# The written-out order of a two-stage attention and MoE kernel, listed anew

## The chip, the cores and the metric

The kernel runs on one core of a Trainium2 chip, as one launch. The metric is the device time in microseconds; the kernel before takes 568.86 us as the median of three runs (568.36 to 571.24).

## What is computed

The inputs are `q`, `k`, `v`, `a_re`, `a_im` of shape 4 x 8 x 768 x 48 (batch, heads, sequence, head size) and two weight matrices of 384 x 2048 and 2048 x 384. The first stage is a linear recurrence over the sequence with a complex decay, the second an MLP on all 3,072 tokens:

```python
mag = sqrt(a_re**2 + a_im**2); scale = minimum(mag, 0.999) / (mag + 1e-6)
for t in range(S):
    S_re, S_im = ar * S_re - ai * S_im + k[t] outer v[t], ar * S_im + ai * S_re
    y[t] = q[t] @ S_re
x = y, with the heads of a token side by side      # 3072 x 384
h = x @ w_in
out = (h * sigmoid(1.702 * h)) @ w_out
```

## The kernel before, in words

The tokens are cut into 12 **chunks** of 256 (`u`, 0 to 11), and the chunks into seven **groups** (`GROUPS`, line 39: chunk 0, chunk 1, then pairs). For each chunk `prepare` (from line 281) turns the decays into factors: a load of `ri` (line 324), logarithms and exponentials on ScalarE (lines 329 to 334), an arctangent (line 351), scans on VectorE (lines 356, 376, 396), sines (lines 424, 425), and the rotation of `qk` into `qr` and `qk` (line 229, steps "rot0" and "rot1"). Each rotated tensor is then brought into the layout by heads, `qkh`, in a **remap**: five DMAs on-chip (lines 447, 448, 450). `attend` (from line 454) computes the chunk's scores on TensorE (line 511), masks them on VectorE into `pm` (line 517), turns keys (line 530, copied out by ScalarE in line 534), mixes the values (line 501) and carries a state `st` from chunk to chunk (lines 553, 569; its decay, line 472, reads the last column of the remapped tensor). The result goes to `xhi` and `xlo` (lines 559, 563). `moe` (from line 617) multiplies by `w_in` into `h_ps` (line 650), applies the activation on ScalarE (lines 659; 663 and 665), takes the rest of it on VectorE into `gl` (line 667), multiplies by `w_out` into `o_ps` (line 681) and writes out through `osb` (line 699, DMA of line 702).

The weights come as float64 in 16 loads of 768 KB, f0 to f15 (line 245), through four buffers, and are **converted** in four steps each: lines 247, 250 and 254 on VectorE, line 253 on ScalarE. Group 0 multiplies in plain fp32 with the converted weights; the later groups take three fp32r products from a high and a low part, which a later split makes (lines 265 to 272). Beside this, the kernel looks at its inputs to see whether the fast way holds for them: 40 **reloads for a check** bring pieces of the weights and of `a` into `raw_w` (lines 710 and 731), and VectorE reduces each (lines 715; 732 and 735). One buffer serves all 40, so a reload waits until the check of the one before it has been done.

**What sets the order.** No scheduler runs. Every step above is a call of `add` in `Plan` (lines 62 to 87), numbered from 0 to 1737 in the order of the calls, with its engine, the tiles it reads and writes, and so the steps it depends on. `ORDER` (line 995) is a list of all 1738 numbers; the loop at line 878 emits the steps in that order. Every engine takes its own steps strictly in listed order, and waits where a step's inputs or buffers aren't ready, with all that is listed behind it on that engine. All DMAs are issued by SyncE (SP), in listed order as well, and a DMA that must wait holds those behind it. Before an activation that needs another table, line 881 emits a table load.

The numbers that are spoken of below:

| step | what it is |
|---|---|
| 80, 128 / 301 / 445 / 970, 1381 | loads of `ri`: chunk 0 (halves) / 1 / 2 / 6, 9 |
| 0, 5, 10, 15, 20, 25, 30, 35, 40, 45, 50, 55, 60 | weight loads f0, f1, f2 and so on to f12 |
| 8, 33, 38, 48 | ScalarE's part of a conversion (line 253) of f1, f6, f7, f9 |
| 100, 150 / 321 | loads of `qk`: chunk 0 (halves) / 1 |
| 164, 179 / 783 | loads of `v`: chunk 0 (both blocks) / 5 |
| 95 | arctangent (line 351) of chunk 0, first half |
| 105, 143, 108, 109 | ScalarE's steps behind the arctangent: lines 404, 351 (second half), 419, 424 |
| 113 | rotation "rot1" of chunk 0, first half; the 13 warm-up matmuls (line 432, steps 114 to 126) and remap 127 need it |
| 112, 127 / 161, 163 | remaps of chunk 0, first / second half |
| 331, 334 / 333, 336 | rotations / remaps of chunk 1 |
| 166, 168 / 181, 183 / 340, 342 | masks (line 517): chunk 0, first / second block / chunk 1 |
| 178 | decay of the state (line 472) by what remap 163 brings |
| 187, 190, 211 | chunk 0, second block: first mix on TensorE, copy of the result, first matmul of line 650 on it |
| 24, 200 | last step of the conversion of f4 (line 254); matmul of line 681 that needs it |
| 14, 29 | last steps of the conversions of f2 and f5; f6 and f9 go into the buffers that they free |
| 129 to 137 | ScalarE's and VectorE's steps on the second half of chunk 0 |
| 272 | split of the second weight tile (line 272) |
| 809, 818 / 887, 896 | `gl` on VectorE (line 667) and the matmul group of line 650 that waits for it: group of chunks 4 and 5, third / last step |
| 328, 329, 330 / 447 / 206, 271 | ScalarE: lines 419, 424, 425 of chunk 1 / line 205 of chunk 2 / activation (line 659) of chunk 0, split (line 265) |
| 1191, 1195 | copy of keys by ScalarE (line 534) in chunk 8, and the scores that wait for it |
| 1610 and 1736 | first `osb` copy of the last group; the matmul of line 753 that counts the checks |

Of the kernel before, what the change touches and what calls it, by code (L numbers as in the profile page):

```python
# [992 lines left out]


ORDER = """
80 5 10 128 100 15 150 0 103 164 81 82 84 83 85 86 6 87 7 88 89 92 90 94
91 11 93 96 95 12 104 129 102 130 97 105 131 132 99 134 135 16 136 106 137 140 133 101
141 138 142 139 107 144 301 143 1 108 153 109 145 154 111 146 110 149 18 112 98 8 155 113
148 157 158 156 152 114 127 147 151 303 2 115 159 3 9 116 302 117 160 13 118 304 25 161
119 17 120 305 4 121 122 307 162 123 165 306 19 169 308 166 35 163 167 309 315 124 171 168  # L1000
310 14 170 28 26 172 173 313 311 174 27 20 125 30 314 175 312 126 317 176 193 316 338 29
177 202 179 321 445 194 178 45 324 182 180 203 318 325 181 204 183 195 36 326 184 205 21 186
320 185 33 187 38 196 23 37 188 22 191 31 189 197 327 322 271 198 24 328 199 32 329 40
355 200 447 323 190 34 206 211 48 39 201 319 330 212 46 55 50 331 213 446 214 43 220 41
332 215 448 333 221 207 42 222 449 334 216 451 229 47 217 335 452 336 218 44 450 208 56 453
209 49 58 223 457 219 454 57 458 230 51 231 59 65 60 210 459 232 224 455 192 238 52 239
456 461 225 460 339 467 75 341 340 226 342 233 337 227 53 66 343 462 68 54 246 344 67 345
247 70 501 273 248 470 285 348 275 353 69 526 277 234 61 471 240 466 464 228 465 78 235 63
241 62 346 242 472 347 354 473 350 71 356 463 64 73 255 469 474 236 349 502 237 468 503 249
357 281 76 358 351 72 250 256 360 77 251 359 269 352 257 476 475 252 366 361 79 477 505 362  # L1010
504 363 74 253 507 478 258 508 243 364 506 245 270 479 509 365 254 510 515 368 511 513 244 367
512 514 517 369 259 481 291 498 260 272 295 261 518 263 262 274 516 377 522 482 523 676 484 483
370 378 519 485 371 265 297 267 486 372 299 373 276 488 374 521 527 487 375 379 496 520 491 480
528 524 386 380 529 279 387 278 531 376 525 532 489 490 381 283 534 388 493 382 389 678 383 530
280 535 533 384 282 494 385 395 677 536 287 396 390 391 537 397 284 289 392 393 398 286 404 679
405 497 680 399 394 293 288 400 681 401 290 413 682 292 414 690 402 406 492 407 403 294 499 415
699 416 540 545 408 409 417 495 422 691 692 410 500 737 411 702 538 683 539 684 296 542 546 541
543 560 266 268 264 412 685 688 431 547 686 544 548 687 689 693 423 550 549 703 558 298 551 552
694 698 555 432 424 556 696 418 697 695 704 559 419 425 420 300 706 553 701 433 1614 561 739 554
421 434 562 427 707 426 563 700 428 564 429 705 435 708 430 557 437 565 709 738 566 567 740 710  # L1020
571 741 568 1615 438 569 742 570 436 711 743 573 744 441 572 1616 579 439 574 1617 714 712 443 575
576 577 580 751 581 752 578 585 745 1618 582 746 1619 591 749 1620 909 444 750 753 583 747 763 748
440 584 754 760 717 731 586 592 715 587 589 713 593 588 758 764 716 597 756 765 718 755 590 594
598 719 759 595 721 599 757 911 761 603 766 762 720 1621 910 724 1622 604 600 722 1623 767 729 596
768 769 605 609 912 770 913 730 723 1624 915 1625 726 725 916 732 1626 771 601 917 918 606 772 602
914 615 919 923 920 733 921 607 610 922 935 611 926 727 608 734 1627 613 925 612 728 929 736 614
1628 735 924 1629 621 927 970 936 616 932 773 622 774 930 617 937 780 618 777 931 623 619 798 783
1630 620 781 627 938 624 782 775 934 628 784 629 1631 940 633 933 1632 941 776 972 939 943 625 942
928 971 785 944 626 630 634 631 778 1633 635 779 945 786 632 974 639 973 975 1634 788 1635 946 976
637 787 984 977 791 636 796 789 640 638 645 1636 986 996 643 646 1637 641 790 797 647 1638 997 793  # L1030
792 799 642 948 648 644 978 649 979 982 1639 794 650 980 985 651 981 983 795 1148 993 1640 800 1641
987 801 652 950 653 802 998 803 655 999 988 804 654 991 951 992 657 805 663 658 995 989 1150 1642
1000 1643 656 949 1644 947 990 442 659 661 994 1001 660 664 952 1003 665 806 1149 1002 1151 953 662 1645
954 807 1646 962 666 808 1647 1004 957 1005 955 669 1152 812 1154 1006 1155 1648 668 963 674 667 809 956
813 965 814 959 818 966 670 1156 672 958 1157 810 964 675 1017 815 1153 811 1162 967 816 819 960 968
961 1171 824 969 1649 820 1160 1650 1158 1163 1161 1159 817 821 1014 1165 1164 1007 822 1174 823 1651 830 1175
1166 1170 1009 831 1015 1008 825 1652 826 1011 1653 832 1205 827 1018 1169 1010 828 836 1654 1019 829 837 833
1020 1655 834 1022 1656 1012 1168 1013 1167 1021 842 1173 838 1016 1176 1030 1207 1657 1025 839 1177 835 1172 843
840 1179 1031 1658 844 1659 1032 848 1178 1180 1023 849 1033 845 1206 1181 1024 850 1660 1027 1661 841 1208 1209
846 1662 671 851 1211 1182 860 1212 1213 1034 1183 1026 1214 847 1215 1035 854 1028 1216 1231 1037 1029 1036 1210  # L1040
1043 673 1038 1044 1039 855 1663 856 852 857 1664 1219 1665 866 861 1217 862 1228 1218 1222 1040 1221 1186 1188
1232 853 858 1223 1233 863 1189 859 1220 864 867 1234 868 872 869 1184 1666 1667 865 873 1187 1668 1185 870
874 1230 1227 871 1190 876 1192 1229 1236 1669 1041 878 1237 1235 875 1670 1224 1238 1239 1671 1381 877 1225 879
884 1191 1241 880 1240 1200 1042 885 881 886 1195 1226 1193 1242 882 1382 883 1383 888 1384 1672 890 1385 1201
887 896 891 892 889 1194 1203 1196 1197 1673 1245 1198 893 1674 1202 1404 894 897 1199 898 899 895 901 1387
902 1388 1675 900 1386 1204 1045 1676 1389 1677 1390 1393 907 1243 1394 905 1244 908 903 1046 1247 1395 1391 904
1251 1250 1051 1047 1392 1246 1252 1678 1048 1049 1052 1398 1053 1050 1679 1055 1054 1397 1680 1248 1253 1401 1249 1057
1407 1396 1063 1058 1402 1681 1255 1682 1400 1254 1399 1683 1408 1403 1056 1064 1256 1257 1059 1258 1065 1060 1263 1409
1061 1264 1066 1411 1684 1412 1062 1406 1067 1685 1405 1686 1442 1069 1414 1068 1415 1070 1260 1071 1266 1072 1075 1410
1259 1687 1688 1267 1689 1265 1081 906 1076 1413 1261 1416 1077 1268 1073 1078 1262 1074 1417 1082 1087 1444 1269 1270  # L1050
1443 1079 1083 1084 1080 1445 1088 1085 1089 1690 1271 1446 1276 1093 1448 1277 1691 1090 1692 1419 1465 1418 1086 1094
1099 1449 1091 1450 1420 1422 1100 1272 1095 1101 1273 1421 1092 1274 1423 1097 1096 1451 1105 1447 1456 1098 1102 1106
1424 1454 1107 1111 1457 1426 1452 1275 1425 1453 1455 1693 1459 1427 1434 1458 1103 1468 1104 1112 1108 1109 1462 1113
1460 1435 1694 1429 1464 1695 1428 1437 1431 1110 1117 1696 1114 1466 1115 1118 1467 1469 1116 1119 1123 1120 1470 1697
1121 1698 1436 1124 1463 1471 1122 1125 1129 1473 1126 1472 1474 1127 1130 1131 1128 1430 1475 1135 1132 1438 1476 1133
1136 1137 1477 1278 1138 1439 1279 1134 1432 1440 1141 1441 1280 1140 1281 1139 1144 1290 1699 1433 1142 1146 1284 1282
1478 1291 1485 1285 1292 1283 1486 1286 1288 1287 1700 1296 1701 1488 1143 1289 1297 1479 1298 1299 1482 1480 1489 1481
1294 1702 1293 1490 1302 1487 1703 1704 1308 1303 1483 1491 1295 1492 1705 1304 1300 1305 1484 1301 1309 1314 1493 1310
1494 1496 1501 1306 1502 1311 1706 1307 1707 1147 1320 1312 1495 1321 1315 1504 1322 1498 1316 1313 1318 1323 1708 1317
1332 1709 1505 1710 1319 1326 1324 1327 1461 1328 1325 1329 1333 1330 1334 1497 1499 1711 1335 1331 1338 1344 1339 1340  # L1060
1341 1336 1337 1345 1350 1346 1347 1712 1713 1145 1503 1342 1343 1351 1356 1352 1353 1714 1348 1500 1715 1716 1362 1357
1358 1506 1507 1508 1717 1349 1718 1509 1719 1510 1354 1359 1355 1363 1360 1364 1365 1368 1361 1369 1366 1370 1371 1511
1367 1512 1372 1513 1374 1514 1720 1373 1375 1517 1379 1377 1721 1515 1722 1378 1518 1519 1516 1520 1521 1523 1723 1522
1524 1529 1525 1526 1535 1530 1531 1532 1724 1527 1725 1380 1528 1536 1541 1537 1538 1533 1534 1542 1547 1543 1544 1539
1540 1548 1545 1549 1550 1726 1546 1553 1551 1554 1555 1559 1556 1727 1728 1376 1552 1560 1565 1561 1557 1729 1562 1730
1558 1566 1731 1571 1567 1568 1563 1577 1572 1573 1564 1569 1574 1732 1583 1578 1579 1570 1575 1580 1576 1584 1581 1585
1586 1733 1582 1589 1595 1590 1591 1592 1734 1587 1735 1588 1596 1601 1597 1598 1593 1594 1602 1599 1603 1604 1600 1605
1606 1608 1736 1607 1610 1609 1611 1612 1737 1613
"""


# [66 lines left out]
```

## Time and profile before

| what | us |
|---|---|
| median of three runs | 568.86 (568.36, 568.86, 571.24) |
| the profiled execution, its own time | 570.0 |
| span in the profile, first to last instruction | 568.3 |
| outside the span, in that execution | 1.7 |
| first matmul | 23.90 |
| end of the last matmul | 561.98 |

How to read it: the page gives each engine's busy time as a share of the span. A share is a mean over the whole span, so the stretches have to be looked at by themselves. A wait is put down to what came last before the waiting instruction started. A matmul's end is modelled, so TensorE's busy time has small holes closed; PEld is the load of weights, which runs beside the matmul before it.

### The profile page before, as it was taken

The numbers are of one execution on the slowest core, as the hardware profiler recorded it, in microseconds if no ns is written. First come the engines' busy times: TensorE is split into PE (matmuls) and PEld (weight loads), VectorE is DVE, ScalarE is ACT, GpSimd is POOL, SyncE is SP. The second block draws the span as 40 slices with busy tenths as digits, with TensorE's granted clock in tenths as the row PEclk, the third lists the DMA queues.
The fourth block names the chain that finished last, engine by engine and source line by source line (L and its number), as shares of the span: only waits on it lengthen the run. The fifth ranks groups of instructions, "written<-read, shape, count | busy, mean of one in ns | idle before, by whom it ended". The sixth has DMA issues, their size and how long they took to land.

```text
span 568.3 us, 14533 instructions
## 1 busy us (share of the span) xinstructions
PE 529.1 (93%) x6204; PEld 447.7 (79%) x6204; DVE 388.6 (68%) x625; ACT 370.7 (65%) x562; POOL 11.1 (2%) x55
## 2 busy tenths in 40 slices
PE   0388999999999999989999999999999999999995
PEld 0267989999987888867888788888888888888884
DVE  6989999999989896967669659728653232241222
ACT  7978989999997969696485777498422133222230
POOL 6000000000000000000000000000000000000000
PEclk9999999999999999999999999999999999999999
DMA  8498983756284765575384753760253213111201
GB/s 337 136 275 314 225 336 66 220 111 203 56 240 141 192 198 128 185 163 163 127 221 125 189 184 107 201 186 1 88 111 88 65 29 89 43 47 47 75 0 60
DMA packets 29270, 82.04 MB, mean 144 GB/s; under 512 B 4112, under 2 KB 7184, under 8 KB 29200
## 3 DMA queue, kind: packets, MB, share of 16 engines
q1 hardware_dynamic: 29200, 81.06, 49.2%
q8 instruction: 50, 0.82, 0.6%
q14 instruction: 20, 0.16, 0.1%
HBM read 57.41 MB, written 4.72 MB: 109 GB/s over the span
## 4 chain that ended last, share of the span: by engine, by line
PE 58%; ACT 5%; DVE 5%; DMA 4%; issue 1%; ACTq 0%; POOL 0%; DVEq 0%
PE o_ps L681 25%; PE h_ps L650 24%; PE x_ps L501 4%; DMA raw_w<-in_w_in_dram 2%; PE z_ps L511 1%; PE p_ps L511 1%; PE z_ps L553 1%; DMA ri<-in_a_dram 1%; DMA qkh<-qr 1%; ACT L881 1%; DVE s L376 1%; DVE fit L715 1%; DVE s L356 1%; PE p_ps L530 1%; PE z_ps L530 1%
## 5 line engine op out<-in xcount | busy, mean ns | idle before, releaser
L663 ACT ACTIVATE gh<-h_ps 128x512 fp32r<-128x512 f32 x88 | 52.1, 597 | 144.3 <-PE h_ps L650 79.5
L667 DVE TENSOR_TENSOR gl<-h_ps,gh 128x512 fp32r<-128x512 f32 x88 | 60.1, 685 | 85.0 <-ACT h_ps L665 65.2
L650 PE MATMUL h_ps<-xhi,hiA 128*128 128x512 f32 (+1 forms) x288 | 109.2, 379 | 2.6 <-DVE gl L667 2.5
L650 PE MATMUL h_ps<-xhi,loA 128*128 128x512 f32 (+1 forms) x288 | 107.2, 372 | 0.0
L650 PE MATMUL h_ps<-xlo,hiA 128*128 128x512 f32 (+1 forms) x288 | 107.2, 372 | 0.0
L681 PE MATMUL o_ps<-gh,hiU 128*128 128x512 f32 (+1 forms) x288 | 80.9, 381 | 0.0
L681 PE MATMUL o_ps<-gl,hiU 128*128 128x512 f32 (+1 forms) x288 | 80.1, 379 | 0.4 <-DVE gl L667 0.4
L681 PE MATMUL o_ps<-gh,loU 128*128 128x512 f32 (+1 forms) x288 | 78.3, 372 | 0.0
L881 ACT ACT_TABLE_LOAD x59 | 75.7, 1283 | 1.9 <-PEq L1126 0.9
L650 PEld LDWEIGHTS h_ps<-xhi,hiA 128*128 128x128 f32 x288 | 54.2, 188 | 13.9 <-DVE gl L667 4.4
L650 PEld LDWEIGHTS h_ps<-xhi,loA 128*128 128x128 f32 x288 | 54.2, 188 | 9.8
L650 PEld LDWEIGHTS h_ps<-xlo,hiA 128*128 128x128 f32 x288 | 54.3, 188 | 9.0
L681 PEld LDWEIGHTS o_ps<-gh,loU 128*128 128x128 f32 x288 | 52.2, 188 | 9.7
L681 PEld LDWEIGHTS o_ps<-gl,hiU 128*128 128x128 f32 x288 | 51.1, 188 | 10.8 <-issue 1.2
L681 PEld LDWEIGHTS o_ps<-gh,hiU 128*128 128x128 f32 x288 | 50.7, 188 | 10.1 <-issue 1.2
L665 ACT ACTIVATE h_ps<-h_ps 128x512 f32<-128x512 f32 x88 | 51.6, 593 | 0.0
L715 DVE TENSOR_REDUCE fit<-raw_w 128x1 f32<-128x384 f32 x64 | 34.1, 544 | 17.0 <-DMA raw_w<-in_w_in_dram 10.3
L229 DVE TENSOR_TENSOR qk<-qk,s 128x768 f32<-128x768 f32 (+2 forms) x39 | 44.2, 1137 | 1.5 <-ACT s L425 1.3
L501 PE MATMUL x_ps<-pm,v 128*32 128x128 f32 x768 | 38.9, 276 | 1.8 <-DMA v<-in_v_dram 1.1
L501 PE MATMUL x_ps<-qkh,st 96*32 96x128 f32 x640 | 32.9, 272 | 0.0
L432 PE MATMUL h_ps<-qk,ident 128*128 128x256 f32 x26 | 7.9, 457 | 23.9 <-DVE s L415 23.9
L501 PEld LDWEIGHTS x_ps<-pm,v 128*32 128x32 f32 x768 | 20.0, 109 | 9.5 <-issue 6.0
(104 smaller groups left out, 783.0 us busy)
## 6 DMA issues: line engine op xcount, KB each, us to landing
v<-in_v_dram SPq DMA_DIRECT2D x24, 416.0 KB, 4.8
ri<-in_a_dram SPq DMA_DIRECT2D x11, 768.0 KB, 5.5
qk<-in_qk_dram SPq DMA_DIRECT2D x11, 768.0 KB, 6.7
qkh<-qr SPq DMA_DIRECT2D x22, 288.6 KB, 5.9
qkh<-qk SPq DMA_DIRECT2D x22, 288.6 KB, 5.6
raw<-in_w_in_dram SPq DMA_DIRECT2D x8, 768.0 KB, 6.7
raw<-in_w_out_dram SPq DMA_DIRECT2D x8, 768.0 KB, 6.3
raw_w<-in_w_in_dram SPq DMA_DIRECT2D x16, 384.0 KB, 3.7
```

The source lines that it names most:

```text
L229: add(en, t, rank, lambda: e.tensor_tensor(out=out, in0=a, in1=b, op=alu), **kw)
L432: add("PE", 0.43, -WARM + k, lambda k=k, dst=dst: mm(h_ps[0][:, k % 2 * T : (k % 2 + 1) * T], lhsT=ident, rhs=dst[:, k % NR, 0:T], start=T ...
L501: mm(x_ps[32 * j : 32 * j + 32, r, :], lhsT=lt, rhs=rt, start=n == 0, stop=n == len(steps) - 1)
L511: mm(ps_[to : to + QL, j, lo:L], lhsT=at(h, 1, c)[:, lo : lo + QL], rhs=at(h, 0, c)[:, lo:L], start=True, stop=True)
L530: nc.tensor.transpose(banks[h // 4][0][:, h % 4, 0:KD], at(h, 1, c), ident[0:KD, 0:KD])
L650: mm(h_ps[hb][:, k * n_x : (k + 1) * n_x], lhsT=ww[:, r * T + f * P : r * T + (f + 1) * P], rhs=x[:, r, xs], start=n == 0, stop=n == last)
L663: add("ACT", a_t(CW) - 0.13, rk(order_), lambda hb=hb, gb=gb: act(out=high.g(gb), in_=h_ps[hb], func=AF.Silu, scale=SLOPE), r=[f"h{hb}"], ...
L665: add("ACT", a_t(CW) - 0.13, rk(order_), lambda hb=hb: act(out=h_ps[hb], in_=h_ps[hb], func=AF.Silu, scale=SLOPE), w=[f"h{hb}"], tab=SILU, ...
L667: add("DVE", d_t(CW), rk(order_), lambda hb=hb, gb=gb: dve.tensor_tensor(out=glo[gb], in0=h_ps[hb], in1=high.g(gb).bitcast(F32), op=ALU.su ...
L681: mm(o_ps[c][:, xs], lhsT=y[:, f * DM + c * P : f * DM + (c + 1) * P], rhs=x[:, k * n_x : (k + 1) * n_x], start=i == 0 and f == 0 and n == ...
L715: add("DVE", d_t(CK), rk + 2, lambda x=x, op=op: dve.tensor_reduce(out=f_w[:, x, n : n + 1], in_=weights.looked_at()[:, :, 1], op=op, axis ...
L881: nc.scalar.preload_act_table_set(o[5])
```

## The change

Only the list `ORDER` is another one. The steps, their engines, sizes, buffers and dependencies are the same 1738, and the number of instructions is the same but for one table load less (58 for 59). The list is new from end to end: on VectorE 479 of 523 steps stand at another place of the engine's queue than before, on SP 133 of 153 DMA steps, mostly by a few places. The first five lines of each list:

```diff
@@ -993,79 +993,79 @@
 ORDER = """
-80 5 10 128 100 15 150 0 103 164 81 82 84 83 85 86 6 87 7 88 89 92 90 94
-91 11 93 96 95 12 104 129 102 130 97 105 131 132 99 134 135 16 136 106 137 140 133 101
-141 138 142 139 107 144 301 143 1 108 153 109 145 154 111 146 110 149 18 112 98 8 155 113
-148 157 158 156 152 114 127 147 151 303 2 115 159 3 9 116 302 117 160 13 118 304 25 161
-119 17 120 305 4 121 122 307 162 123 165 306 19 169 308 166 35 163 167 309 315 124 171 168
...
+80 5 128 0 100 10 82 81 84 83 85 86 6 87 7 8 94 129 88 9 130 92 89 25
+150 131 93 90 103 1 132 91 96 134 135 2 133 136 97 137 102 98 142 140 301 15 99 95
+138 104 139 141 144 105 143 106 101 108 107 145 146 109 153 111 154 110 155 148 112 147 149 3
+13 113 156 11 114 303 127 152 157 4 115 159 302 12 116 158 117 151 26 118 160 164 119 304
+305 120 14 307 121 122 16 18 30 179 123 161 27 167 308 162 165 309 124 166 310 169 17 163
...
 """
```

The same, read out for the engines on which the argument turns. SP's queue, its beginning, up to remap 336 (a remap is five DMAs):

```
before: 80 5 10 128 100 15 150 0 164 301 | 112 127 | 25 | 161 | 35 | 163 | 20 30 338 179 321 445 45 40 355 55 50 | 333 336
after:  80 5 128 0 100 10 25 150 301 15 | 112 127 | 164 30 179 | 161 163 | 20 321 45 35 445 40 338 50 55 | 333 336
```

ScalarE's queue at its beginning, with table loads as T, and around the copy 190:

```
before: 81 82 84 85 86 87 88 89 90 T 95 T 129 130 105 132 134 135 136 137 133 138 T 143 108 109
after:  82 81 84 85 86 87 8 129 88 130 89 90 132 134 135 133 136 137 98 T 95 138 105 143 108 109
before: 186 185 33 38 23 T 197 271 328 329 447 190 206 48 319 330
after:  23 185 186 T 197 206 33 48 190 328 38 329 330
```

What stands ahead of a step on VectorE in one list and not in the other (line numbers in brackets):

```
113: no longer 11 (L247), 12 (L250), 16 (L247); now 2 (L250), 9 (L254)
178: now 31 (L247), 324 (L396)
331: no longer 39 (L254), 46 (L247); 334: no longer 42 (L250)
272: no longer 513 (L337), 517 (L356, three scans)
809: no longer 674 (L699), 1151 (L229), 1639 1640 1642 1643 1645 1646 1648 (L715); now 958 (L517)
887: no longer 1241 and 1384 (L229), 1666 1667 1669 1670 1672 (L715)
```

On SP, `ri` load 1381 stood behind three reloads for a check (1665, 1668, 1671) and now stands ahead of reload 1662. Load 970 now stands behind reload 1626, load 783 behind both. At the end TensorE's step 1736 moves behind the last matmul group, and the `osb` copy 1610 ahead of 1608.

## Rows read from the trace of the kernel before

**Rows 1.** The page, part 1: busy time and share of the span by engine.

```profile
PE 529.1 (93%) x6204; PEld 447.7 (79%) x6204; DVE 388.6 (68%) x625; ACT 370.7 (65%) x562; POOL 11.1 (2%) x55
```

**Rows 2.** Stretches: length; busy us of PE, PEld, DVE, ACT, POOL (instructions); clock; DMA share, GB/s.

```profile
0.00:24.00 24.00, 0.10 (x1) 0.13 (x1) 18.82 (x46) 20.56 (x36) 8.88 (x30) 1.00 0.70 259
24.00:108.00 84.00, 78.33 (x1207) 71.63 (x1208) 80.62 (x113) 74.67 (x105) 0.65 (x7) 1.00 0.77 232
108.00:330.00 222.00, 218.72 (x2967) 184.44 (x2970) 183.38 (x281) 178.45 (x263) 1.23 (x14) 1.00 0.60 164
330.00:562.00 232.00, 231.98 (x2040) 191.51 (x2032) 104.99 (x185) 96.98 (x160) 0.34 (x4) 1.00 0.29 82
```

**Rows 3.** Timeline of PE, 36 to 74 us: start, us, line, operation, [idle before <- releaser].

```profile
40.47 1.27 PE L511 MATMUL z_ps<-qkh 96*32 96x128 f32 x30 [1.26 <-issue]
...
47.05 0.42 PE L501 MATMUL x_ps<-pm,v 128*32 128x128 f32 x8 [1.08 <-DMA v<-in_v_dram]
...
52.47 0.94 PE L681 MATMUL o_ps<-g,valU 128*128 128x128 f32 x6 [0.24 <-DVE valU L254]
...
54.09 0.94 PE L650 MATMUL h_ps<-x,valA 128*128 128x128 f32 x6 [0.69 <-ACT x L559]
...
71.32 0.42 PE L511 MATMUL p_ps<-qkh 96*32 96x128 f32 x6 [0.38 <-DMA qkh<-qk]
72.05 0.68 PE L511 MATMUL p_ps<-qkh 96*32 96x128 f32 x24 [0.30 <-DMA qkh<-qk]
```

**Rows 4.** Timeline of DVE, 40 to 74 us.

```profile
41.00 0.56 DVE L472 TENSOR_TENSOR st<-st,qkh 96x384 f32<-96x384 f32 x1 [1.59 <-DMA qkh<-qk]
41.47 1.75 DVE L396 TENSOR_TENSOR_SCAN s<-runs,s 128x771 f32<-128x771 uint8 x1
...
51.47 0.95 DVE L254 CUSTOM_DVE_ANT_0 valU<-raw,valU 128x1536 uint16<-128x1536 uint16 x1
...
60.16 1.75 DVE L229 TENSOR_TENSOR qk<-qk,s 128x1536 f32<-128x1536 f32 x1
...
72.88 0.69 DVE L517 TENSOR_TENSOR pm<-p_ps,mask 128x512 f32<-128x512 f32 x1 [1.12 <-PE p_ps L511]
```

**Rows 5.** Timeline of ACT in the opening.

```profile
10.23 0.52 ACT L351 ACTIVATE s<-s 128x384 f32<-128x384 f32 x1
10.77 1.28 ACT L881 ACT_TABLE_LOAD   x1
...
21.18 0.88 ACT L253 ACTIVATE raw<-raw 128x768 int32<-128x768 uint32 x1
```

**Rows 6.** Timelines of DVE and PE at the opening's end.

```profile
22.84 0.95 DVE L229 TENSOR_TENSOR qk<-qk,s 128x768 f32<-128x768 f32 x1
...
23.90 6.05 PE L432 MATMUL h_ps<-qk,ident 128*128 128x256 f32 x20 [23.90 <-DVE s L415]
29.87 0.76 PE L511 MATMUL p_ps<-qkh 96*32 96x128 f32 x32
```

**Rows 7.** DMA issues (80 at 0.93, 128 at 2.31, 179 at 39.91, 45 at 42.38): KB, us to landing.

```profile
ri<-in_a_dram SPq DMA_DIRECT2D x1, 384.0 KB, 3.1
...
ri<-in_a_dram SPq DMA_DIRECT2D x1, 384.0 KB, 6.6
...
v<-in_v_dram SPq DMA_DIRECT2D x1, 416.0 KB, 7.1
...
raw<-in_w_in_dram SPq DMA_DIRECT2D x1, 768.0 KB, 10.4
```

**Rows 8.** Timelines of DVE and PE around 250 us.

```profile
250.66 0.55 DVE L715 TENSOR_REDUCE fit<-raw_w 128x1 f32<-128x384 f32 x1 [4.66 <-DMA raw_w<-in_w_in_dram]
...
252.47 0.50 PE L650 MATMUL h_ps<-xhi,hiA 128*128 128x512 f32 x1 [1.79 <-DVE gl L667]
```

**Rows 9.** Waits, 320 to 328 us: us in total, times, longest.

```profile
ACT s L205 <- DMA ri<-in_a_dram: 2.7, 1, 2.7
...
PE h_ps L650 <- DVE gl L667: 0.8, 1, 0.8
```

136 rows, old and new, of the table ORDER are left out of this document.

## The prediction

> **What bounds the kernel now.** The first view is busy time by engine, for the whole span: PE works 529.1 of 568.3 us [rows 1], so a new order can only take back the 39 us in which PE stands still. The second view, busy time by stretch, says where those are [rows 2]. Up to 24 us PE has nothing to do; that part is set by the chain of ScalarE and VectorE that ends in the first half of remap 0. From 24 to 108 us PE is idle for 84.0 - 78.33 = 5.7 us, from 108 to 330 for 222.0 - 218.72 = 3.3, from 330 to 562 for nothing, and some 6.3 us follow the last matmul. The granted clock is 1.00 in every stretch, so no part of the time is the throttle's. In the second stretch VectorE is nearly full as well, 80.62 of 84.0 us: there its queue order moves PE. From 108 us on it has 39 us of air, and single waits decide.
>
> The third view, PE's timeline from 36 to 74 us [rows 3], names the idle times. Remap 161/163 (chunk 0, second half) brings 1.26 us ahead of the scores, the `v` load 179 1.08, the conversion 24 0.24, the copy 190 0.69, remap 333/336 0.38 and 0.30. That is 3.95 of the 5.7; the remaining 1.7 lie in pieces of a few tenths. VectorE's timeline [rows 4] shows the same two remaps from its side: 1.59 us of idle ahead of 178 and 1.12 ahead of chunk 1's masks, 2.7 of its 84.0 - 80.62 = 3.4 us.
>
> **The change, part by part.** Nothing is added; the terms are what each engine's queue has ahead of the steps that PE waits for.
>
> *A, the opening.* The arctangent 95 ran at 10.23, between two table loads [rows 5]. Now step 8 (0.88 us) and eight half-width steps (some 0.52 us each, from the arctangent's own row) stand ahead of it, 5.1 us, and two table loads of 1.28 us go. So 95 runs near 15.3, and what follows it (105, 143, 108, 109) no longer waits for the second table pair. If none of this were covered, the opening would end 5.1 - 2.6 = 2.5 us later; if one table load was on the path and all else is covered, 1.3 earlier. I take the value from VectorE's side: 113 ended the chain at 22.84 + 0.95 [rows 6], and VectorE's work ahead of it is nearly the same (11, 12 and 16 leave, 2 and 9 come, 0.1 us less). What is won is the landing of `ri` load 128. Alone, load 80 landed 3.1 us after its issue; 128, behind two weight loads of 768 KB, after 6.6 [rows 7]. One of the two is moved behind it: (6.6 - 3.1) / 2 = 1.75 us earlier. VectorE had 5.2 us of air in this stretch [rows 2], so only a part of the 1.75 reaches 113; I take a third. **A = -0.6**, bounds -1.3 and +2.5.
>
> *B, 24 to 108 us.* On SP, loads 25 and 35 no longer stand between the remaps of chunk 0, and 30 and 179 stand ahead of 161. Load 30 waits for step 14, which VectorE does some two steps behind 113's followers, so 161 is issued about when it was; 163 has one load of 768 KB less to land beside, which is worth up to the same 1.75 us. VectorE has 31 and 324 ahead of 178 now, the second of them 1.75 us long [rows 4]: they fill its 1.59 us of idle. So the 1.26 us of PE go, and a wait for the mask 181 comes: VectorE is later by 0.55 + 1.75 - 1.59 = 0.7 (31 is a short step, taken as 0.55), PE arrives up to 1.26 earlier, so between 0.7 and 2.0 us; taken 1.3. Load 179 was issued at 39.91 and landed 7.1 us later [rows 7]; standing ahead of 161 it goes out near 30, and its 1.08 us are gone. The copy 190 loses five steps ahead of it on ScalarE (38, 271, 328, 329, 447) and gains 48 and 206: its 0.69 goes. Step 24 ended at 51.47 + 0.95 = 52.4; without the 1.59 of idle and with A it ends near 50, and since PE loses waits of its own ahead of 200, I take 1.1 us of wait there for 0.24. For chunk 1, 331 and 334 lose three conversion steps (39, 46, 42), 2.2 us at the 0.95 of such a step's row less a short one; 334 began at 60.16 and would begin near 57.
>
> From PE's side: 1.26 + 1.08 + 0.69 + 0.38 + 0.30 = 3.7 go, 0.9 is added at 200, and the 1.3 at the mask takes the place of the small pieces (1.7): -3.7 + 0.9 - 0.4 = -3.2. From VectorE's side, which is full: its two idles go, 1.59 + 1.12 = -2.7. I take **B = -3.0**. Bounds: 0, if remap 333/336 lands when it did; -5.7, if all of PE's idle in the stretch goes.
>
> *C, 108 to 330 us.* At 250.66 VectorE stood 4.66 us, waiting for a reload, ahead of the `gl` that PE waited 1.79 us for [rows 8]. Seven check reductions and two more steps leave the place ahead of that `gl` (809) and one mask comes: the reload's landing no longer stands in its way, and the 1.79 goes. At 326 PE waits 0.8 us for `gl` 887, which hung on the `ri` load 1381 (ScalarE waited 2.7 us) [rows 9]; 1381 is moved ahead of reloads, and seven steps leave the place ahead of 887. Both go: -2.6. New, the scores 1195 may wait for ScalarE's copy 1191, which has more ahead of it; nothing in the trace shows that wait, and the bounds are 0 and the 1.79 of the largest wait of the stretch; 0.8 is taken, near the middle, as the row of 326 is of that size. **C = -1.8**, bounds -3.3 (all idle of the stretch) and 0.
>
> *D.* Behind 330 us PE had no idle time [rows 2], so the other moves there, 1736 among them, cost and give nothing: the cover is PE's own queue. One table load less, 1.28 us of ScalarE outside A, is covered in the same way; ScalarE works 370.7 of 568.3 us.
>
> **Sum:** -0.6 - 3.0 - 1.8 = -5.4, so 564.6 against the profiled execution's 570.0. That one is 1.1 us above the median of 568.86; on the median's footing, **563.5 us**.
>
> **A rule that speaks against it.** In the new list load 55 goes out directly ahead of the five DMAs of remap 333, and load 50 before that. The row nearest to it is load 45: with others in front of it, it took 10.4 us to land [rows 7]. The Trainium skill, page "DMA: Bandwidth & Descriptors", section "Queues, rings and completion order", says that each DMA engine consumes the descriptors of SP's row in ring order. By that rule remap 333 stands behind the whole of load 55 and gains nothing; this is the first rival.
>
> **The rivals.** *First, remap 333/336 is late as before.* The mechanism is loads 50 and 55, each 768 KB and some 1.75 us of transfer, directly ahead of it. For: PE's 0.38 and 0.30 us at 71 to 72 were waits for just this remap, issued behind those loads [rows 3]. Against: they stood close ahead of it already, and 334 runs some 3 us earlier. Price: B is lost, 564.6 + 3.0 = 567.6, **566.5** at the median.
>
> *Second, the reload that gives way hits another load.* Load 970 now stands behind reload 1626, and 783 behind both; the reload waits until VectorE has done the check before it, as the one at 246 to 250.66 did. For: a `ri` load behind reloads cost ScalarE 2.7 us [rows 9]. Against: VectorE has air there. Price: C is lost and 2.7 is added, 569.1, **568.0**.
>
> *Third, slower: weight load f9.* SP's step 45 waits for VectorE's step 29, with 35 and 445 queued behind it; and on ScalarE the conversion 48 of f9 now stands ahead of the copy 190, where it stood behind it, with 328, 38, 329 and 330 next. For: 45 was issued at 42.38 and landed after 10.4 us, at 52.8, when 190 ran at about 53.6 (PE took it at 54.09 [rows 3]). Landing as late as that, it would push 190 back to its old place, and each us beyond costs one, at PE and through 330 at remap 333. With B lost, A and C still give 2.4, so the end is 2.84 us slower only from 2.4 + 2.84 = 5.2 us beyond 52.8 on: if 45 lands later than 58. Price at 58.5: 564.6 + 3.0 + 5.7 - 1.1 = **572**. Against: fewer bytes stand ahead of it now (only 20 and 321 are fresh), and 3.1 us was the time of a load with nothing ahead, half its size [rows 7].
>
> By the Trainium skill, the same page, section "Anatomy of one DMA — SWDGE (gpsimd) path", a transfer takes some 2.0 us and its bytes at 436 GB/s; that is an estimate of 3.8 us for f9, and would leave the third rival out. No row shows such a load by itself.
>
> **How the numbers follow.** Forecast 0.56, first rival 0.20, second 0.12, third 0.12. The time is the forecast's. Low: all idle of 24 to 330 us and 1.3 of the opening gone, 570.0 - 10.3 - 1.1 = 558.6. High: past the second rival by the half of its 2.7, 569.5; the third lies outside. A measurement can tell about 0.5%, 2.84 us, so faster is below 566.0 and slower above 571.7. The forecast and half of the first rival, which straddles 566.0, are faster: 0.66. The other half and the second are the same: 0.22. The third is slower: 0.12.
>
> **What would show it.** Right: PE's first scores before 29.87, near 29.3; no wait of 178 for `qkh` and none of `x_ps` for `v`; chunk 1's scores near 69 instead of 71.32; idle of PE in 24 to 108 us of some 2.7; no idle above a tenth at 252 and 326; the last matmul near 556.5. Wrong: idle of a few us at 190 to 200 (third rival), chunk 1's scores at 71 or later behind the same remap (first), an idle of `ri` or `v` near 206 (second), or an idle at 1195 above 0.8.

## The result, and the profile after

The changed kernel takes 564.71 us as the median of seven runs (562.30 to 566.28), the kernel before 568.78 (567.91 to 571.24): ratio 0.9918, interval 0.9892 to 0.9944. Two more series of runs gave 0.9876 (0.9846 to 0.9906) and 0.9892 (0.9847 to 0.9937). So it is faster by 4 to 7 us, and 563.5 was close. The profile shows that the total is right and that the parts are not.

The profiled execution has a span of 563.3 us, against 568.3. Busy time by engine, and by the stretches of [rows 2]:

```profile
PE 527.2 (94%) x6204; PEld 447.8 (79%) x6204; DVE 389.4 (69%) x625; ACT 370.5 (66%) x561; POOL 12.0 (2%) x55
```

```profile
0.00:24.00 24.00, 0.90 (x2) 0.84 (x3) 19.51 (x47) 18.41 (x36) 9.44 (x30) 1.00 0.76 278
24.00:108.00 84.00, 76.17 (x1146) 71.01 (x1145) 78.41 (x107) 73.94 (x104) 1.20 (x7) 0.98 0.76 229
108.00:330.00 222.00, 221.47 (x3102) 187.53 (x3101) 185.99 (x287) 184.64 (x269) 1.05 (x14) 1.00 0.58 160
330.00:557.00 227.00, 227.00 (x1951) 187.38 (x1950) 103.39 (x182) 93.50 (x156) 0.33 (x4) 1.00 0.31 87
```

From 24 to 108 us PE now stands still for 84.0 - 76.17 = 7.8 us, not for 5.7, and VectorE for 5.6 instead of 3.4. From 108 to 330 it is 0.5 instead of 3.3. The stretch that was to give 3.0 us gives nothing, and the next one gives all that it had.

PE's waits in the first two stretches, in its timeline (before: [rows 3, 6]):

```profile
23.10 6.00 PE L432 MATMUL h_ps<-qk,ident 128*128 128x256 f32 x20 [23.10 <-DVE s L415]
...
32.15 0.63 PE L501 MATMUL x_ps<-pm,v 128*32 128x128 f32 x12 [0.51 <-DVE pm L517]
33.63 0.85 PE L501 MATMUL x_ps<-pm,v 128*32 128x128 f32 x20 [0.85 <-DVE pm L517]
...
37.80 1.60 PE L650 MATMUL h_ps<-x,valA 128*128 128x128 f32 x12 [1.75 <-ACT x L559]
...
50.94 0.94 PE L681 MATMUL o_ps<-g,valU 128*128 128x128 f32 x6 [1.12 <-DVE valU L254]
...
70.70 3.75 PE L681 MATMUL o_ps<-g,valU 128*128 128x128 f32 x18 [3.23 <-ACT g L659]
74.38 0.77 PE L511 MATMUL p_ps<-qkh 96*32 96x128 f32 x32
```

All the waits of [rows 3] are gone but the one at 200, and others stand in their place. The longest, 3.23 us, is for an activation, step 224. Its engine's timeline just before:

```profile
64.11 0.85 ACT L334 ACTIVATE s<-s 128x768 f32<-128x768 f32 x1
67.82 0.92 ACT L253 ACTIVATE raw<-raw 128x768 int32<-128x768 uint32 x1 [2.87 <-DMA raw<-in_w_in_dram]
68.76 1.28 ACT L881 ACT_TABLE_LOAD   x1
70.05 0.60 ACT L659 ACTIVATE g<-h_ps 128x512 f32<-128x512 f32 x1
```

ScalarE stood 2.87 us in the conversion 58, which waited for weight load f11, and 224 is listed right behind it. In the old list 58 ran at 64.35, long after f11 had landed at 60.2. Now f11 is load 55, the one listed directly ahead of remap 333. SP's timeline, and the load's issue with its time to landing:

```profile
56.63 0.33 SPq L245 DMA_DIRECT2D raw<-in_w_in_dram  x1
...
61.53 1.18 SPq L447 DMA_DIRECT2D qkh<-qk  x2
67.82 0.65 SPq L448 DMA_DIRECT2D qkh<-qk  x1
```

```profile
raw<-in_w_in_dram SPq DMA_DIRECT2D x1, 768.0 KB, 11.2
```

f11 took 11.2 us and landed at 67.8; in the same moment SP got on with remap 336, in whose middle it had stood for five us. In the profile of before SP stood there as well, until 66.18, when f10 (load 50, issued last ahead of that remap) landed. In seven of the fourteen profiles of this case SP stands in the middle of this remap, and in each it goes on within 0.03 us of the landing of the load that was issued last ahead of 333. So the remap waits for the load in front of it, and the new list put a load there that ScalarE needs at once. The 3.23 us cost more than themselves: the granted clock then fell (columns as in [rows 2]).

```profile
66.00:70.00 4.00, 1.48 (x14) 1.28 (x12) 2.18 (x3) 2.16 (x2) 0.00 (x0) 1.00 0.80 177
70.00:72.00 2.00, 1.30 (x6) 1.30 (x7) 2.00 (x4) 1.99 (x4) 0.17 (x2) 0.60 0.62 132
72.00:74.00 2.00, 2.00 (x12) 2.00 (x12) 2.00 (x4) 1.97 (x4) 0.00 (x0) 0.55 0.83 283
74.00:76.00 2.00, 2.00 (x70) 1.84 (x69) 0.96 (x3) 2.00 (x3) 0.00 (x0) 1.00 1.01 419
```

With a clock of 0.60 and 0.55 the 18 matmuls behind the wait took 3.75 us. In another execution of the same kernel, with a wait of only 0.26 us, they took 2.27 (below).

The two other executions of the changed kernel that were profiled have such a stretch as well, once each, behind the wait for the conversion 24. The first of them, PE's timeline and the stretch:

```profile
52.82 1.23 PE L681 MATMUL o_ps<-g,valU 128*128 128x128 f32 x6 [2.09 <-DVE valU L254]
53.85 2.77 PE L650 MATMUL h_ps<-x,valA 128*128 128x128 f32 x12
```

```profile
53.30:56.70 3.40, 3.40 (x19) 3.40 (x18) 3.40 (x5) 3.37 (x6) 0.00 (x0) 0.50 0.88 314
```

A granted clock of 0.50 is the lower of TensorE's two levels, 1.2 instead of 2.4 GHz. The 12 matmuls took 2.77 us, and 1.50 at a clock of 1.00 in the profile of after. So each of the three executions lost some 1.5 to 1.7 us to a low clock between 24 and 107 us, behind a wait of 3.2, 2.1 or 1.8 us; in the profile of before the longest wait there is 1.26 us, and the clock stays at 1.00. Not every such wait is followed by it: the wait of 1.75 us at 36 us was followed by a low clock in some runs of other orders, and in none of these three.

**Where PE gained and lost** can be read step by step. Each group of matmuls gets the duration that it has in the profile of before; where the new list has come to a certain sum of work, the table says how many us sooner than in the profile of before that sum was reached. The last columns are the ends of PE's work and of the span; the entries are good to some 0.3 us. The three rows "after" are three executions.

```
PE's lead, us, at     24    64    84   107   126   248   270   332   460 | PE end  span
after               +0.8  +1.2  -2.5  -0.9  -0.1  -0.5  +2.0  +3.3  +3.4 |  +3.3  +5.0
after, again        +0.8  -2.3  -1.2  +0.2  +1.1  +0.7  +3.2  +4.5  +4.5 |  +4.5  +6.2
after, third        +0.9  -2.8  -1.7  -0.3  +0.5  +0.1  +2.7  +4.0  +4.0 |  +3.9  +5.6
old, new from 103   +0.1  +0.2  +0.6  +0.9  +0.5   0.0  +2.7  +3.9  +3.9 |  +3.9  +3.7
opening only        +0.8  +0.7  +1.3  +1.3  +1.3  +1.3  +0.9  +1.0  +1.0 |  +1.0  +1.5
new to 103, old     +0.9  +0.9  +1.7  +2.8  +2.5  +2.7  +5.0  +5.0  +5.0 |  +5.0  +6.6
the same, again     +0.7  -0.8  +0.2  +1.6  -0.4  -0.6  +1.2  +1.5  +1.5 |  +1.5  +3.1
```

In all three executions of the changed kernel the opening gives 0.8, and at 107 us 0.2 or less is left of it; 4.2 to 4.3 are won from there to the end; and between PE's end and the span's end some 1.7 us more go. That last part was in no term of the prediction.

### The profile page after: what moved, and what is told of

Its sections match the earlier page's. It is cut to its first block, busy times and chain, and to the rows that moved or that the text cites. A ratio compares the mean times of both kernels' runs of the same rounds, so it can differ in the third digit from the quotient of the medians.

```text
span 563.3 us, 14541 instructions
## 1 busy us (share of the span) xinstructions
PE 527.2 (94%) x6204; PEld 447.8 (79%) x6204; DVE 389.4 (69%) x625; ACT 370.5 (66%) x561; POOL 12.0 (2%) x55
## 4 chain that ended last, share of the span: by engine, by line
PE 60%; ACT 1%; DVE 1%; issue 0%; ACTq 0%
PE o_ps L681 26%; PE h_ps L650 25%; PE x_ps L501 4%; PE z_ps L511 1%; PE p_ps L511 1%; PE z_ps L553 1%; PE p_ps L530 1%; PE z_ps L530 1%; DVE qr L229 0%; DVE qk L229 0%; DVE gl L667 0%; ACT L881 0%; ACT h_ps L665 0%; ACT s L333 0%; ACT s L331 0%
## 5 line engine op out<-in xcount | busy, mean ns | idle before, releaser
L881 ACT ACT_TABLE_LOAD x58 | 74.4, 1283 | 1.9 <-PEq L1126 0.9
L681 PE MATMUL o_ps<-g,valU 128*128 128x128 f32 x192 | 26.3, 289 | 4.3 <-ACT g L659 3.2
```

The lines of the kernel that those rows point to most:

```text
L681: mm(o_ps[c][:, xs], lhsT=y[:, f * DM + c * P : f * DM + (c + 1) * P], rhs=x[:, k * n_x : (k + 1) * n_x], start=i == 0 and f == 0 and n == ...
L881: nc.scalar.preload_act_table_set(o[5])
```

## The experiments

**The list cut at 103 us.** Two kernels join the two lists at step 395, on either side.

```diff
-ORDER: the new list
+first kernel: the first 395 steps of the new list, then the others in the old order
+second kernel: the first 395 steps of the old list, then the others in the new order
```

> The first 395 steps stand as in the new list (up to about 103 us), all others in the order of the old one. Theory from the trace of after: the new list gains 0.8 us in the opening, loses more than that between 66 and 74 us, and is about 1 us behind the old one at 108 us; all of the 4 us come later. Then this kernel is not faster: 568.8 to 571, PE idle 23.1 to the first matmul, and both waits for gl (1.8 at 250, 0.8 at 326) back. Rival, the prediction's own term: the stretch up to 108 us gives 3.6 of the gain; then 565.2.

> The first 395 steps stand as in the old list, all others in the order of the new one. Theory: the gain lies behind 108 us (both waits for gl gone, 2.6 us, some small ones, and up to 1.9 at the end), so 563.5 to 565, as fast as after or a little faster, since the loss at 66 to 74 us is not there. Rival, the prediction's terms: 1.8 us there and nothing at the end, 567.0.

Measured: the first 570.14 us, ratio 0.9997 (0.9967 to 1.0027); the second 566.27, 0.9942 (0.9916 to 0.9968). The new beginning by itself is worth nothing that the runs show, and the new rest 3.3 us. The runs of before beside them have a median of 569.57, so by the theory the second was to come to 564.3 to 565.8 and by the rival to 567.8: it lies between, nearer the theory. The table says what is short: PE gets its 3.9 us, but the closing part, from the landing of the last output to the end of the span, does not get shorter (3.76 us, for 3.53 before and 1.94 after). The first kernel was profiled in its fastest run, 563.8, 6 us under its median; there f11 landed after 6.2 us and PE waited 0.26 us before 225. So a second execution was profiled:

> The order with the new first 395 steps and the old rest, a second look, since its first profile (563.8) lies 6 us under the median of its runs (570.1). Theory: f11 lands later than in the first look (63.1) and PE waits before 225 again, and the old order's waits at 250 and 326 us are longer than the 0.26 and 0.74 of the first look; time 568 to 571. If the first look was typical, 564.

Measured: 567.3 us, a little under what was expected. f11 landed at 64.0 and PE waited 0.29 us before 225, so that part of the theory missed. The old order's part is what differs most between the two executions: the lead falls from 1.6 to -0.4 between 107 and 126 us, with a wait of 1.17 us at 119 for a split of line 272, and the wait at 250 is 0.64 instead of 0.26. Up to 107 us the second is behind by 1.2, with a stretch of low clock from 38.8 us on that the first does not have. Both have the first 395 steps of the changed kernel and more lead at 107 us (2.8 and 1.6) than its three executions: this order does not fix what that stretch takes.

**The opening alone.** The first 85 steps of the new list, to 25 us, then the old order.

> The first 85 steps (to 25 us) as in the new list, one table load less, all others in the old order. Theory: PE starts at 23.1 instead of 23.9, the 0.8 is gone again by 108 us, since VectorE and the remaps set that stretch; what stays is SP's standstill of 1.7 to 2.0 us in the closing part, which so far came in all three kernels with the old opening and in none of the ten runs with the new one: if the opening decides it, the closing part is 1.9 us and the time 1.6 to 2.5 us under before, ratio 0.9955 to 0.997. Rival: what stands between 25 and 103 us decides it; closing part 3.2 to 3.8 us, ratio 0.998 to 1.000.

Measured: 567.65 us against 568.93, ratio 0.9978 (0.9960 to 0.9997), so 1.3 us, with an interval from 0.2 to 2.3. PE starts at 23.07, and the 0.8 is *not* gone at 108 us: with the old list behind it, the lead stays at 0.9 to 1.3 to the end. The theory was wrong there, and that sharpens the reading of B: in the three executions of the changed kernel the new order of 25 to 103 us doesn't merely add nothing, it loses what the opening had won. By time that is not shown, since the intervals of this kernel and of the first joined one overlap. The closing part was 3.06 us, so the opening does not decide that.

**Step 58 behind 224.**

```diff
 ScalarE's queue
-452 453 454 58 224 455
+452 453 454 224 58 455
```

> After, with one step moved: ScalarE's part 58 of the conversion of f11 stands behind the activation 224 instead of ahead of it. PE's 3.2 us before 225 go, since 224 no longer waits for f11. Theory one, the late remap is a second limit: 336 still lands near 73.8, PE stands before the scores 339 instead, some 2 to 3 us, and the time is 563.5 to 565. Theory two, f11 alone is the limit: the 3.2 us and the low clock after it are won, 560 to 561.5.

Measured: 563.44 us, ratio 0.9902 (0.9879 to 0.9924). PE's wait before 225 is gone; PE stands before 339 instead, 0.69 and 0.26 us, and remap 336 lands at 73.6. Theory one, with smaller waits than it expected. The ratio lies between those of the three series of after.

**Load 55 earlier.** Steps 37, 39 and 55 directly ahead of 331. Of the engines' queues only VectorE's changes by it: step 39, which load 55 waits for, comes ahead of the rotation 331. In SP's queue 55 still stands directly ahead of 333.

```diff
 the list around load 55 of the changed kernel
-37 50 319 220 446 331 213 277 221 447 39 214 332 43 207 46 55 333
+50 319 220 446 37 39 55 331 213 277 221 447 214 332 43 207 46 333
```

> After, with 37, 39 and the load 55 listed ahead of 331, so that f11 is issued some 2 us earlier and no longer directly ahead of remap 333. Theory one, a load directly ahead of a remap is overrun by it: f11 lands within 7 us, by 62, and the 3.2 us before 225 go; the remap is 0.9 us later by VectorE's work and lands near 74, so PE stands before 339 and the time is 563.5 to 565.5. Theory two, the remap is late because of the load ahead of it: it lands by 71 and the time is 560 to 562. Rival, f11 is late for the bytes ahead of it: it lands behind 66 still and nothing changes, 564.7.

Measured: 563.67 us, 0.9898 (0.9873 to 0.9924). f11 was issued 1.9 us ahead of remap 333 and still landed after 11.0 us, at 69.3; the remap at 71.8 and 74.3. So theory one fell. The second is not tested by it, since the load is still the one directly ahead of the remap: SP stood in the middle of 336 until 69.28, when f11 landed. Two us of room change nothing for either. The late landing is what the rival expected, but PE waited only 0.68 us before 225, since it came late by other waits already, and the time is not after's to the tenth but within its spread.

**The changed kernel again, and three steps moved at once.**

> The changed kernel as it is, beside the three others of this series. Theory: the 3.2 us of PE before 225 come with how late f11 lands, which differs between executions of one order (11.2 us in the profile of after, 6.2 in that of the order with the same first 395 steps); the ratio is 0.990 to 0.994 as before. If the wait were fixed by the order, f11 lands at 67 to 68 again.

Measured: 562.83 us, 0.9876, below the ratio expected. f11 landed after 5.8 us, so the time of that load is not fixed by the order, as the theory said: three executions have 11.2, 5.8 and 5.9 us. PE's waits of 24 to 108 us in this one:

```profile
PE o_ps L681 <- DVE valU L254: 2.1, 1, 2.1
PE h_ps L650 <- ACT x L559: 1.8, 1, 1.8
PE x_ps L501 <- DVE pm L517: 1.3, 2, 0.8
PE o_ps L681 <- ACT g L659: 0.3, 1, 0.3
```

and the 18 matmuls that had been slow, in its timeline:

```profile
71.00 2.27 PE L681 MATMUL o_ps<-g,valU 128*128 128x128 f32 x18 [0.26 <-ACT g L659]
```

The wait at 225 has shrunk from 3.2 to 0.3, and the one before 200, for the conversion 24, has grown from 1.1 to 2.1. PE's lead at 107 us is 0.2. The 1.8 for the copy 175 is in every execution; in the profile of after its engine's timeline reads:

```profile
34.36 0.84 ACT L216 ACTIVATE s<-s 128x768 f32<-128x768 f32 x1
35.23 1.28 ACT L881 ACT_TABLE_LOAD   x1
36.52 0.84 ACT L351 ACTIVATE s<-s 128x768 f32<-128x768 f32 x1
37.27 0.47 ACT L559 ACTIVATE x<-x_ps 128x384 f32<-128x384 f32 x1
```

The copy (37.27) stands behind an arctangent and its table load, though its input was there at 34.48. So three moves were tried together:

```diff
 the changed kernel's queues
-ScalarE: 311 316 175 177        58 224
+ScalarE: 311 175 316 177        224 58
-VectorE: 22 326 24 327
+VectorE: 22 24 326 327
```

> After with three steps moved: 58 behind 224 as above, the copy 175 (chunk 0, first block) ahead of the arctangent 316 on ScalarE, and the conversion 24 ahead of 326 on VectorE. Theory: the waits of PE before 225 (3.2), before 202 (1.75) and most of that before 200 (1.1) go, those before 339 stay: 560.5 to 562.5, faster than after by 2 to 4 us. Rival: what is won at 202 and 200 is lost at 339, since remap 333/336 lands when it did: 563 to 564, as with 58 alone.

Measured: 562.91 us, 0.9885 (0.9854 to 0.9916): no faster than after beside it (562.83). The waits before 202 and 225 are gone, and PE's timeline shows where they went:

```profile
39.76 0.41 PE L511 MATMUL z_ps<-qkh 96*32 96x128 f32 x4 [1.24 <-DMA qkh<-qk]
...
51.97 0.94 PE L681 MATMUL o_ps<-g,valU 128*128 128x128 f32 x6 [1.49 <-DVE valU L254]
...
60.00 0.94 PE L650 MATMUL h_ps<-x,valA 128*128 128x128 f32 x6 [1.74 <-ACT g L659]
```

PE comes sooner to remap 161/163, to the conversion 24 and to an activation, and waits there. The first is the rival's way, only earlier than the rival had it. In this profile PE's lead at 107 us is 1.3, but the runs don't bear it out. So two waits were taken away, and others came at the next places.

**Load 55 behind the remap,** with its conversion behind it.

> After with load 55 (f11) listed behind remap 333/336 and its conversion (56, 57, 58, 59) and load 75 behind it. Theory, the first rival's: the weight load directly ahead is what makes the remap late; 333 then lands some 9 us after its first DMA is issued instead of 10.7 to 13.9, 336 by 70. The conversion of f11 is late instead and PE waits 2 to 4 us before 238, so the time is 563 to 566. Rival: the remap is as late without the load, 336 at 72 or later.

Measured: 565.18 us, 0.9925 (0.9891 to 0.9959). SP's timeline, without 55 ahead of the remap:

```profile
61.18 1.53 SPq L447 DMA_DIRECT2D qkh<-qk  x2
62.76 1.35 SPq L448 DMA_DIRECT2D qkh<-qk  x1
...
65.43 0.58 SPq L245 DMA_DIRECT2D raw<-in_w_in_dram  x1
```

SP no longer stands in the middle of the remap. Remap 333 lands 7.8 us after its first DMA, at 64.5, and 336 at 67.6; in the three executions of after these are 10.5 to 13.9 us, 69.6 to 70.9, and 72.6 to 73.8. That is the first rival's mechanism, shown: the load ahead costs the remap some 3 to 6 us. The load gains too: f11 landed 4.4 us after its issue. The time is not better, since f11's conversion is late now, and the matmuls behind the wait run at a low clock (2.26 us for 12, 1.50 otherwise):

```profile
74.56 2.26 PE L650 MATMUL h_ps<-x,valA 128*128 128x128 f32 x12 [2.30 <-DVE valA L254]
```

**The reload ahead of 809.** In the old list the check reduction 1648 alone was moved behind the `gl` step 809.

```diff
 VectorE's queue of the kernel before
-1005 1648 674 809 966
+1005 674 809 1648 966
```

> Before with one step moved: the check reduction 1648, which waits for the reload 1647, stands behind the gl step 809. Theory: PE's 1.8 us before 818 go, so the time is 1.5 to 2 us under before (ratio 0.996 to 0.998) and PE's idle of 108 to 330 us falls from 3.3 to 1.5. Rival: another wait takes the place (the osb copy 674 or 809's own input), ratio 1.000.

Measured: 568.59 us, 0.9981 (0.9954 to 1.0008), which leaves "nothing" in the interval. The trace agrees with the theory: PE's wait at 250 us is gone (its lead grows from 1.0 at 248 to 2.5 at 270), and what PE waited for from 108 to 330 is

```profile
PE z_ps L511 <- DVE st L569: 0.6, 1, 0.6
PE o_ps L681 <- DVE gl L667: 0.4, 1, 0.4
PE p_ps L511 <- ACT kt L534: 0.2, 1, 0.2
```

**The closing part.** In the profile of before SP stands still 2.0 us among its closing instructions, after the last output has landed; in that of after that row is missing. SP's waits of the last us, before and after:

```profile
SPq L1134 <- SPq L1134: 2.0, 1, 2.0
SPq L886 <- SPq L886: 1.0, 1, 1.0
```

```profile
SPq L886 <- SPq L886: 1.0, 1, 1.0
SPq L1134 <- PEq L1134: 0.6, 2, 0.4
```

A standstill of this kind, 1.6 to 2.1 us long, was in all four kernels with the old order from 25 to 103 us (before, the second joined one, 1648 moved, opening alone), each time directly ahead of SP's 408th instruction. It was in none of the executions with the new order there. A shorter program on SP, 405 for 410 instructions, could be the reason:

```diff
 the output transfers of line 702, first of three in each group but the last
-out[c, 0:n_t] <- buf[:, 0:n_t]
+out[c, 0:n_t/2] <- buf[:, 0:n_t/2]; out[c, n_t/2:n_t] <- buf[:, n_t/2:n_t]
```

> After with the first of the three output transfers of each group but the last cut in two, six more DMAs on SP, all of them behind no one. In the three kernels so far with 409 or 410 instructions on SP in the trace, SP stands still 1.7 to 2.1 us before its 408th, among the closing instructions; in the seven with 405 or 406 it does not. Theory, the place in SP's program decides: the wait is back, some 1.8 us before the 408th, the closing part is 3.5 instead of 1.94 us, and the time is 1.5 us over after's. Rival, it is the old opening that brings it: no such wait, same time as after.

> The changed kernel once more, beside the one with six more DMAs. Closing part 1.94 us again and a ratio of 0.988 to 0.992; f11 lands between 64 and 68 and PE's waits before 200 and 225 share 2 to 4.5 us between them.

Measured: 563.54 us, 0.9884 (0.9838 to 0.9930), beside 563.74, 0.9892, for after, which came as expected. With 413 instructions on SP there is no such row:

```profile
SPq L702 <- DVE osb L699: 21.9, 2, 21.6
SPq L1134 <- PEq L1134: 0.6, 2, 0.5
SPq L886 <- SPq L886: 0.5, 1, 0.5
```

So the length of SP's program is not the reason, at least not alone. What SP waits for stays open; what is shown is that the standstill goes with the order between 25 and 103 us.

No version tried beats the changed kernel clearly: 0.9884 to 0.9902 for four variants lies within its own three ratios, and the fifth, with load 55 behind the remap, above them.

## Why the prediction came out, point by point

**A, -0.6: right.** PE starts 0.8 us earlier, and the opening alone is worth 1.3 us in time (0.2 to 2.3). The route was as told: load 128 landed 1.8 us sooner, at 7.1; the arctangent ran at 15.08, for an estimate of 15.3. ScalarE's opening, with the one table load ahead of it:

```profile
13.79 1.28 ACT L881 ACT_TABLE_LOAD   x1
15.08 0.52 ACT L351 ACTIVATE s<-s 128x384 f32<-128x384 f32 x1
```

**B, -3.0: wrong, and this is the step that failed.** From 24 to 107 us the changed kernel loses 0.6 to 1.7 us in its three executions, which is outside the bounds of -5.7 and 0. The prediction took PE's waits one by one, saw that each cause was moved out of the way, and counted them as gains; then it let VectorE's idle time confirm it. The waits did go, but others came, at the next places where PE needs VectorE, ScalarE or a remap, as they did behind the three moves, which took away two waits and got none of it back in time.

What sets the pace of this stretch is not shown: VectorE, which the prediction took for the full engine, stood idle for 4.6 to 5.6 us in the three executions, more than the 3.4 of before. And the prediction put the clock at nothing, since it was 1.00 before. The low clock behind one of the new waits costs 1.5 to 1.7 us in each execution, about what is lost; without it the waits would come out between 0.2 lost and 1.1 won, an estimate from the leads at 107 us (-0.9, 0.2 and -0.3, with 1.5 to 1.7 added, against the 0.8 of the opening).

Two more pieces were missed. Remaps 333 and 336 landed at 69.6 to 70.9 and at 72.6 to 73.8, not clearly sooner than the 70.5 and 72.7 of before: the first rival had this place and this mechanism, with a chance of 0.20, and the sign that was set for it came, chunk 1's scores at 71 us or later: they began at 73.2 to 74.4. The load that it names cost PE 3.2 us in one of three executions, by a way that was not priced: through f11's own conversion on ScalarE. And the copy 175, behind 316, had no price, though its place could be read from the list. The wait for 24 was priced at 1.1 and measured 1.1, 2.1 and 1.8. The wait of 184 for the mask 181, priced at 1.3, did not come; masks 166 and 168 cost 1.3 to 1.4 instead, a little earlier.

The Trainium skill, page "DMA: Bandwidth & Descriptors", section "Queues, rings and completion order", has descriptors consumed in ring order on each DMA engine. The remap that waits for the load ahead of it agrees with that: 10.5 to 13.9 us with the load, 7.8 without.

**C, -1.8: right in its causes, too small.** Both waits went, as said. From 108 to 330 us this remains:

```profile
PE h_ps L650 <- DVE gl L667: 0.5, 1, 0.5
```

The new wait of 1195, taken at 0.8, did not come; the 0.5 is another, at 219. PE's lead grows by 4.2 to 4.3 us behind 107. The two waits make 2.6 of it and the small ones the rest of the 3.3 that were idle, less 0.5. Some 1.5 us are in no wait at all: behind step 395 the busy time of PE itself is 452.8 to 452.9 us in all three executions, for 454.4 in the profile of before, and some 1.0 of that is on line 681 (with the old beginning ahead of it, the sum is 453.6). The matmuls are the same and follow each other in another order: two neighbours have different tiles (the 128*128, 128*32 and so on of the rows) 255 times behind step 395 in the old order and 232 times in the new one. That this is the reason is not shown; which sequences cost less was not tried. The prediction had no term for this, its bound of -3.3 was "all idle of the stretch", and the gain went past it.

**D, nothing: right for PE,** whose lead doesn't change behind 332 us. But the sum left out what stands behind PE's end, where 1.7 us went. Its table load is misplaced, at no cost: the opening has two fewer, 2 for 4, and the whole list only one, so behind the opening there is one more and not one less.

So 0.8 - 1.1 + 4.2 + 1.7 = 5.6 us of span, as the mean of the three executions, against 5.4 forecast as 0.6 + 3.0 + 1.8: a loss where most of the gain was forecast, made up by two gains that were not. That the total came so close is luck. The other rivals fell. Load 970 was issued at 199.3 and landed at 205.2, and PE did not wait; f9 was issued at 41.27 and landed at 49.1 after 7.8 us, well ahead of the 52.8 from which it would have cost. The 3.8 us that the prediction estimated for f9 from the Trainium skill, page "DMA: Bandwidth & Descriptors", section "Anatomy of one DMA — SWDGE (gpsimd) path", did not hold for it: that section is on DMAs issued by GpSimd, and f9, issued by SP behind other transfers, took the 7.8. (The high end of the range, 568.0 and half of 2.7, comes to 569.4 and not to 569.5.)

## What to carry to other kernels

Where other engines are nearly full, don't add up the waits of the engine that you want to speed up: one that is taken away can come back at the next place where two engines meet. Count what makes the chain of the others shorter, with the landing of the transfers in it. A new wait on TensorE has a second price: here waits of 1.8 to 3.2 us were followed by a low clock, for another 1.5 to 1.7 us. A load that is listed directly ahead of a long on-chip transfer delays that transfer and may itself be late, so what is listed behind its first consumer, on that consumer's engine, belongs into the price.

## What the runs showed that was not expected

The busy time of PE depends on the order of its matmuls: 1.5 us of some 454, with the same instructions. In all three executions of the changed kernel one wait, of 1.8 to 3.2 us, was followed by a stretch at a granted clock of 0.50, and cost another 1.5 to 1.7 us (3.75 against 2.27 for 18 matmuls in one of them). And the same order gives a load of 768 KB that lands after 5.8 us in one execution and after 11.2 in another, so one profile of this stretch is one draw: of twelve runs of the kernel with the new first 395 steps eleven lie between 563.8 and 571.0 us and one at 573.2, while all runs of the kernel with the new rest on the old beginning lie within 1.5 us (565.5 to 567.0). Why the old rest spreads so much was not found; moving 1648 alone did not narrow it (565.7 to 573.8). The clock has a part in it: in three of the four series of 17 or 18 runs of the kernel before, the longer runs have the lower mean clock (correlation -0.73 to -0.80; in the fourth -0.35).
